# A two-layer decode kernel: three quarters of a single-head key cache loaded anew instead of four, PSUM laid out by hand, and the key products of five items shared among three engines

## The chip, the cores and the metric

The kernel runs on one core of one Trainium2 chip. The metric is the device time of one execution in microseconds (us). The kernel before was timed in three runs: 2697.79, 2698.55 and 2700.42 us, so its median is 2698.55 us. An engine is named as in the profile: PE is TensorE, DVE is VectorE, ACT is ScalarE, POOL is GpSimd, and SP is the queue from which almost every DMA is issued.

## The reference

A residual stream of two tokens (batch 2, one position each, 576 wide) goes through the same two blocks twice: attention over a long cache, then a gated GELU block. The weights and the caches are the same in both layers, so each layer reads the whole key and value cache again.

```python
def _A_ref(x, k_cache, v_cache, wq, wo):          # H, Sk, Dh = 32, 8192, 128
    q = (lambda x, *d: x.transpose(*d))((x @ wq).reshape(B, Sq, H, Dh), 0, 2, 1, 3)
    scores = jnp.einsum("bhqd,bhkd->bhqk", q, k_cache) * (Dh ** -0.5)
    p = _softmax(scores, axis=-1)
    o = jnp.einsum("bhqk,bhkd->bhqd", p, v_cache)
    return (lambda x, *d: x.transpose(*d))(o, 0, 2, 1, 3).reshape(B, Sq, H * Dh) @ wo
def _B_ref(x, w_gate, w_up, w_down):
    g = jnp.einsum("bsd,df->bsf", x, w_gate)
    u = jnp.einsum("bsd,df->bsf", x, w_up)
    return jnp.einsum("bsf,fd->bsd", _gelu(g) * u, w_down)
x = A_x
x = x + _A_ref(_layernorm(x, axis=-1), A_k_cache, A_v_cache, A_wq, A_wo)
x = x + _B_ref(_layernorm(x, axis=-1), B_w_gate, B_w_up, B_w_down)
x = x + _A_ref(_layernorm(x, axis=-1), A_k_cache, A_v_cache, A_wq, A_wo)
x = x + _B_ref(_layernorm(x, axis=-1), B_w_gate, B_w_up, B_w_down)
```

Everything is float32. The key cache and the value cache hold 268 MB each.

## The kernel before

**Items and parts.** The attention of a layer is cut into 34 items (lines 60 to 65). Items 0 to 29 are pairs: two heads of one batch element, 8 MB (of 2^20 bytes) of keys and 8 MB of values. Items 30 to 33 (`SINGLE` in the code) are one head each, 4 MB of keys and 4 MB of values. An item is worked through in parts of 1 MB, that is 16 rows of 128 numbers on each of the 128 partitions: 8 parts in a pair, 4 in a single. A part is what the change calls a quarter of a key cache. Layer one takes the items from 0 to 33 (its code calls the layer 0), layer two from 33 down to 0 (layer 1 in the code).

**What a part costs.** `multiply` (line 520) multiplies the part in place by the query on DVE (line 527; the query was copied to all partitions by PE into PSUM, line 507). POOL then adds the right half of each row of 128 to its left half (line 539), and `add_up` (line 541) lets DVE sum the remaining 64 (line 542). In the first six items of layer two only 12 of the 16 rows go that way: ACT sums the other four, row by row (line 532, `own_rows` on line 512). `at_once` (line 516) marks the first and the last part of item 33 in layer two, which skip the POOL step, so that DVE sums whole rows. When `add_up` of a part is done, its place in SBUF is free, and the next load that waits for that place may start.

**Softmax and values.** After an item's last part, `peak` and `highest` find the maximum (DVE, then PE, then DVE, then PE), `softmax` takes the exponentials on ACT, `total` their sum (PE, reciprocal on DVE). `values` (line 617) multiplies the weights with the value cache on PE, 32 matmuls for a single and 64 for a pair, and frees a value part after every four groups of rows. `gather` (DVE), `context` (PE) and `divide` (DVE) make the output row. All of this is issued inside the parts of the next item, in the loop of lines 699 to 742: at k == 0 the last part of the previous item is added up, at k == 1 come `highest` and `softmax`, at k == 2 `total`, `gather` and `values`, at k == 3 `divide`. Each engine executes its own instructions strictly in the order in which they were written.

**Memory.** All loads go to one SBUF tile, `space`, cut into six slots of 4 MB, the last of which lies in a ring of four places. `plan_first`, `plan_second` and `plan_mlp` write down the order of all loads. They go out on SP in just that order, and each waits until what lay in its place is no longer needed. When layer one ends, the keys of items 32 and 33 and the values of items 31, 32 and 33 stay in SBUF for layer two (line 65). `plan_second` (line 343) then loads the query weights, the four key parts of item 31 into the ring, the four of item 30 over the keys of item 33, the values of item 30 over the values of item 33, the keys of item 29 over the keys and the values of item 32, the keys of item 28 in two halves of 4 MB into the slots 5 and 4, and the values of item 29 as one load of 8 MB into the slots 0 and 1. From then on keys and values alternate in loads of 8 MB.

**PSUM.** `acc` takes two of the eight banks of 2 KB per partition. `xps`, `po`, two buffers of `qp` (the query) and two of the small results (tag "small") are tiles of their own.

Of the kernel before, what the change touches and what calls it, by code (L numbers as in the profile page):

```python
# [9 lines left out]
F32 = mybir.dt.float32  # L10
# [112 lines left out]
def decode_layers(ctx, tc, x_in, kc, vc, wq, wo, wg, wu, wd, out):  # L123
# [6 lines left out]
    psum1 = ctx.enter_context(tc.tile_pool(name="psum1", bufs=1, space=PSUM))  # L130
    psum2 = ctx.enter_context(tc.tile_pool(name="psum2", bufs=2, space=PSUM))
    ctx.enter_context(tc.manual_schedule())
# [20 lines left out]
    def done(key):  # L153
        arena.free(key)
        pump()
# [187 lines left out]
    def plan_second():  # L343
        for us in WQ[1]:
            half_rows(("wq", 1, us[0]), wq, us, None)
        last = PAIRS - 1
        k63, v63, k62, v62 = ("k", 1, SINGLE[3]), ("v", 1, SINGLE[3]), ("k", 1, SINGLE[2]), ("v", 1, SINGLE[2])
        for k in range(4):
            one(("k", 1, SINGLE[1]), kc, SINGLE[1], k, None)
        for k in range(4):  # L350
            one(("k", 1, SINGLE[0]), kc, SINGLE[0], k, (k63, k))

        for kind, k in (("v", 0), ("v", 1), ("k", 0), ("v", 2), ("v", 3), ("k", 1), ("k", 2), ("k", 3)):
            if kind == "k":
# [12 lines left out]
        for g in groups(1):  # L367
            out_rows(1, g)
# [72 lines left out]
    nc.vector.memset(xps, 0.0)  # L441


    def norm(split=False):
# [5 lines left out]
        )  # L450
        every4 = psum2.tile([P, 4 * 6], F32, name="every4", tag="small")
        nc.tensor.matmul(every4, same, apart.rearrange("p c t -> p (c t)"), start=True, stop=True)
# [27 lines left out]
    def attention(layer):  # L480
# [13 lines left out]
        qb, S, prod, rs, mT, rinv, osb = {}, {}, {}, {}, {}, {}, {}  # L494
        po = psum1.tile([P, GH, 2], F32, name="po")

# [15 lines left out]
        def own_rows(n):  # L512

            return 12 if layer == 1 and n in seq[:6] else JC

        def at_once(n, k):

            return layer == 1 and n == seq[0] and k in (0, ITEMS[n].parts - 1)

        def multiply(n, k):  # L520

            if k == 0:
                S[n] = work.tile([P, SK * 2 // P], F32, name="S")
# [3 lines left out]
            nc.vector.tensor_tensor(  # L527
                out=u, in0=t, in1=qb[n].unsqueeze(1).to_broadcast([P, JC, DH]), op=ALU.mult
            )
            r = own_rows(n)  # L530
            for j in range(r, JC):
                nc.scalar.activation(  # L532
                    u[:, j, :], u[:, j, :], AF.Copy, accum_out=S[n][:, k * JC + j:k * JC + j + 1]
                )
# [4 lines left out]
            nc.gpsimd.tensor_tensor(out=half, in0=half, in1=u[:, :r, DH // 2:], op=ALU.add)  # L539

        def add_up(n, k):
            nc.vector.tensor_reduce(  # L542
                out=S[n][:, k * JC:k * JC + own_rows(n)], in_=prod.pop((n, k)), axis=AX.X, op=ALU.add
            )
# [6 lines left out]
            if k == ITEMS[n].parts - 1:  # L551
                ready.pop(key)

        def peak(n):
            m = work.tile([P, 1], F32, name="m")
            nc.vector.reduce_max(m, S[n][:, :ITEMS[n].rows], axis=AX.X)  # L556
            mT[n] = psum2.tile([1, P], F32, name="mT", tag="small")
            nc.tensor.transpose(mT[n], m, ident)  # L558

        def highest(n):  # L560

            heads = ITEMS[n].heads
            m1 = work.tile([1, 2], F32, name="m1")
            nc.vector.reduce_max(m1[:, :heads], mT.pop(n).rearrange("p (i q) -> p i q", i=heads), axis=AX.X)  # L564
            mT[n] = psum2.tile([P, 2], F32, name="nb", tag="small")
            nc.tensor.matmul(mT[n][:, :heads], ones[0:1, :], m1[:, :heads], start=True, stop=True)  # L566
# [28 lines left out]
        def total(n):  # L595
            it = ITEMS[n]
            tot = psum2.tile([P, 2], F32, name="tot", tag="small")
            nc.tensor.matmul(tot[:, :it.heads], ones, rs.pop(n), start=True, stop=True)  # L598
# [275 lines left out]
```

## Time and profile before

The profiled execution took 2699.86 us; the span from its first to its last instruction was 2698.0 us.

| | |
|---|---|
| median of three runs | 2698.55 us |
| profiled execution, its span | 2699.86 us, 2698.0 us |
| bytes moved by DMA | 1155.41 MB, mean 428 GB/s |
| DVE busy | 1865.5 us (69%) |
| POOL busy | 1189.3 us (44%) |
| PE busy | 897.0 us (33%) |
| ACT busy | 130.9 us (5%) |

The shares are means over stages that differ: two attention stages of some 1200 us each, and two short blocks of weights. The page has a row that shows for each of 40 slices how busy the 16 DMA engines were and how much they moved; that row is to be read first, then the same for shorter windows, then the instructions inside the windows that stand out.

### The profile page before, as it was taken

What the parts mean: (1) busy time and instruction counts of PE and PEld (TensorE: products, weight loads), DVE (VectorE), ACT (ScalarE), POOL (GpSimd) and SP (SyncE); (2) the same over time, 40 slices, a digit from 0 to 9 for tenths busy, and PEclk for the clock granted to TensorE, in tenths of its full rate; (3) what the DMA queues carried; (4) which work ended last, traced back from release to release, by engine and by line L of the source; (5) the groups of instructions that cost most, each with busy time, mean ns of one, the idle gap of its engine ahead of it and who ended that gap; (6) DMA issues with size and microseconds to landing.
All of it is one profiled execution on the core that took longest, in us unless ns stands there. A gap on an engine that the chain in (4) does not pass through costs nothing.

```text
span 2698.0 us, 18267 instructions
## 1 busy us (share of the span) xinstructions
PE 897.0 (33%) x7020; PEld 293.9 (11%) x7020; DVE 1865.5 (69%) x1688; ACT 130.9 (5%) x657; POOL 1189.3 (44%) x526
## 2 busy tenths in 40 slices
PE   1323332333233223334653332333233323322355
PEld 0100010001000000111211110001000100000022
DVE  4877787678777776876039887778767867787740
ACT  0000000000000000000013100000000000000000
POOL 2644454445445444544015454445444544544420
PEclk7656665665666566666666665666566666656667
DMA  9999999999999999999999999999999999999998
GB/s 420 436 433 433 434 435 433 432 433 435 434 433 433 432 432 432 433 429 422 407 388 409 434 428 433 433 435 431 432 435 434 431 435 432 434 434 434 435 420 379
DMA packets 33687, 1155.41 MB, mean 428 GB/s; under 512 B 4008, under 2 KB 4032, under 8 KB 5824
## 3 DMA queue, kind: packets, MB, share of 16 engines
q1 hardware_dynamic: 33560, 1154.24, 99.5%
q8 instruction: 55, 0.90, 0.1%
q14 instruction: 32, 0.26, 0.0%
q10 hardware_dynamic: 40, 0.01, 0.0%
HBM read 1154.23 MB, written 0.00 MB: 428 GB/s over the span
## 4 chain that ended last, share of the span: by engine, by line
DMA 84%; DVE 13%; PE 2%; issue 1%; POOL 0%; SPq 0%; ACT 0%; ACTq 0%; DVEq 0%; POOLq 0%
DMA space<-in_A_k_cache_dram 75%; DVE space L527 8%; DVE S L542 4%; DMA space<-in_B_w_up_dram 3%; DMA space<-in_A_wo_dram 2%; DMA space<-in_A_v_cache_dram 2%; DMA space<-in_B_w_down_dram 2%; DMA space<-in_A_wq_dram 1%; PE acc L628 0%; POOL space L539 0%; DMA space<-in_B_w_gate_dram 0%; PE acc L782 0%; DMA x<-in_A_x_dram 0%; PE acc L487 0%; PE xps L831 0%
## 5 line engine op out<-in xcount | busy, mean ns | idle before, releaser
L539 POOL TENSOR_TENSOR space<-space 128x1024 f32<-128x1024 f32 (+1 forms) x510 | 1185.3, 2324 | 1269.1 <-DVE space L527 1253.2
L527 DVE TENSOR_TENSOR space<-space,qp 128x2048 f32<-128x2048 f32 x512 | 1166.3, 2278 | 597.1 <-DMA space<-in_A_k_cache_dram 571.8
L628 PE MATMUL acc<-space,prz 128*8 128x512 f32 x4096 | 589.0, 738 | 455.7 <-DMA space<-in_A_v_cache_dram 450.9
L542 DVE TENSOR_REDUCE S<-space 128x16 f32<-128x1024 f32 (+1 forms) x512 | 612.4, 1196 | 3.1 <-POOL space L539 3.1
L558 PE MATMUL mT<-ident,m 128*1 128x128 f32 x68 | 25.0, 367 | 806.0 <-DVE m L556 806.0
L628 PEld LDWEIGHTS acc<-space,prz 128*8 128x8 f32 x4096 | 118.0, 103 | 869.4 <-DMA space<-in_A_v_cache_dram 451.8
L587 ACT ACTIVATE nbs<-nb 64x1 f32<-64x1 f32 (+1 forms) x128 | 21.1, 165 | 2230.7 <-PE nb L566 2230.0
L558 PEld LDWEIGHTS mT<-ident,m 128*1 128x1 f32 x68 | 5.4, 79 | 822.9 <-issue 791.7
L653 PE MATMUL po<-of,osb 128*32 128x2 f32 x512 | 41.0, 202 | 130.8 <-DVE osb L644 130.8
L566 PE MATMUL nb<-m,unit 1*128 1x2 f32 (+1 forms) x136 | 39.4, 357 | 124.9 <-DVE m L564 124.9
L473 POOL TENSOR_TENSOR rstd<-ve,mhalf 128x1 f32<-128x1 f32 x4 | 2.2, 550 | 167.0 <-DVE ve L471 167.0
L644 DVE SCALAR_TENSOR_TENSOR osb<-acc,diag,osb 128x128 f32<-128x128 f32 x192 | 67.4, 351 | 6.8
L807 DVE STREAM_TRANSPOSE o<-o 128x288 f32<-128x288 f32 x4 | 2.8, 693 | 92.4 <-ACT o L805 92.4
L598 PE MATMUL tot<-sums,unit 128*128 128x2 f32 x120 | 35.3, 363 | 91.7 <-ACT prz L589 91.7
L507 PE MATMUL qp<-qsb,pick 4*64 4x128 f32 (+1 forms) x256 | 31.3, 306 | 80.1 <-DVE space L527 76.9
L589 ACT ACTIVATE prz<-S,nbs 64x128 f32<-64x128 f32 (+1 forms) x128 | 50.7, 396 | 11.7 <-POOL prz L579 7.5
L653 PEld LDWEIGHTS po<-of,osb 128*32 128x32 f32 x512 | 35.7, 154 | 139.1 <-DVE osb L644 137.8
L566 PEld LDWEIGHTS nb<-m,unit 1*128 1x128 f32 x136 | 33.5, 304 | 146.3 <-DVE m L564 146.3
L477 DVE TENSOR_TENSOR x<-xps,x 128x144 f32<-128x144 f32 x4 | 1.2, 308 | 69.0 <-PE xps L831 39.1
L532 ACT ACTIVATE space<-space 128x128 f32<-128x128 f32 x128 | 38.0, 297 | 64.5 <-DVE space L527 60.8
L598 PEld LDWEIGHTS tot<-sums,unit 128*128 128x128 f32 x120 | 30.1, 312 | 96.9 <-ACT prz L589 96.9
L782 PE MATMUL acc<-space,xt 128*8 128x288 f32 x288 | 31.4, 581 | 18.4 <-DMA space<-in_B_w_up_dram 10.7
(64 smaller groups left out, 345.6 us busy)
## 6 DMA issues: line engine op xcount, KB each, us to landing
space<-in_A_k_cache_dram SPq DMA_DIRECT2D x6, 4096.0 KB
space<-in_A_v_cache_dram SPq DMA_DIRECT2D x6, 4096.0 KB
space<-in_A_wo_dram SPq DMA_DIRECT2D x15, 1152.0 KB
space<-in_A_k_cache_dram SPq DMA_DIRECT2D x16, 1024.0 KB
space<-in_B_w_gate_dram SPq DMA_DIRECT2D x3, 3456.0 KB
space<-in_A_v_cache_dram SPq DMA_DIRECT2D x10, 1024.0 KB
space<-in_A_wq_dram SPq DMA_DIRECT2D x3, 3072.0 KB
space<-in_B_w_gate_dram SPq DMA_DIRECT2D x16, 576.0 KB
```

The costliest lines, as they stand in the source:

```text
L507: nc.tensor.matmul(qb[n][to, :], pick[32 * c:32 * c + 4, r:r + 1].to_broadcast([4, P // it.heads]), qsb[32 * c:32 * c + 4, (h % 4) * DH:(h ...
L527: nc.vector.tensor_tensor(out=u, in0=t, in1=qb[n].unsqueeze(1).to_broadcast([P, JC, DH]), op=ALU.mult)
L532: nc.scalar.activation(u[:, j, :], u[:, j, :], AF.Copy, accum_out=S[n][:, k * JC + j:k * JC + j + 1])
L539: nc.gpsimd.tensor_tensor(out=half, in0=half, in1=u[:, :r, DH // 2:], op=ALU.add)
L542: nc.vector.tensor_reduce(out=S[n][:, k * JC:k * JC + own_rows(n)], in_=prod.pop((n, k)), axis=AX.X, op=ALU.add)
L566: nc.tensor.matmul(mT[n][:, :heads], ones[0:1, :], m1[:, :heads], start=True, stop=True)
L589: nc.scalar.activation(pr[at, lo:].rearrange("p (g e) -> p g e", e=4)[:, 0:it.rows // 2:2, :], s[at, :it.rows].rearrange("p (g r) -> p g r ...
L598: nc.tensor.matmul(tot[:, :it.heads], ones, rs.pop(n), start=True, stop=True)
L628: nc.tensor.matmul(accumulator(n)[32 * c:32 * c + 8, :], pr[:, at:at + 8], t[g // 4][:, g % 4 * 4:g % 4 * 4 + 4, :].rearrange("p j d -> p ...
L644: nc.vector.scalar_tensor_tensor(t, q[:, r, :], diag[:, r:r + 1], t, op0=ALU.mult, op1=ALU.add,)
L653: nc.tensor.matmul(po[lo:lo + 32, i, :], t[:, i::GH], of, start=True, stop=True)
L782: nc.tensor.matmul(acc[32 * c:32 * c + 4 * B, h, :HG], window(u, 4 * g + 2 * e), w[:, k, c, :], start=(key == steps[0][0] and k == 0), sto ...
```

## The change

It has five parts.

1. While layer one works on item 31, ACT copies the item's last key part into four banks of PSUM (`kept`) before it is overwritten by the products. In layer two only three key parts of item 31 are loaded; when its first part has been added up, ACT copies `kept` into that part's place, and it is used from there as the fourth part.
2. `plan_second` follows: the ring's fourth place takes the first key part of item 30, every later load of the stage is moved up by one place, and the values of item 29 are loaded in two halves, each of which waits for its own slot only.
3. For the first five items of layer two (33, 32, 31, 30, 29) DVE multiplies 12 of the 16 rows of each part; POOL multiplies the other four with a copy of the query that ACT has put in SBUF. ACT now sums seven rows of each part instead of four, and POOL and DVE sum nine instead of twelve (in the two parts done at once: ACT five, DVE eleven). The sixth item, 28, is no longer treated in a special way.
4. PSUM, with four banks gone, is laid out by hand: `xps` and both query buffers share one bank, `po` and both small buffers another. The query of the next item is issued after the first `multiply` of an item instead of ahead of it.
5. Where the item before the current one is a single, `divide` is put off from k == 3 to k == 1 of the next item (`late`); elsewhere it stays at k == 3.

```diff
-        for k in range(4):
+        for k in range(3):
             one(("k", 1, SINGLE[1]), kc, SINGLE[1], k, None)
         for k in range(4):
-            one(("k", 1, SINGLE[0]), kc, SINGLE[0], k, (k63, k))
-        for kind, k in (("v", 0), ("v", 1), ("k", 0), ("v", 2), ("v", 3), ("k", 1), ("k", 2), ("k", 3)):
+            one(("k", 1, SINGLE[0]), kc, SINGLE[0], k, (k63, k - 1) if k else None)
+        one(("k", 1, last), kc, last, 0, (k63, 3))
+        turns = iter(range(1, 5)), iter(range(4))
+        for kind in "vkvvkvkk":
             if kind == "k":
-                one(("k", 1, last), kc, last, k, (k62, k))
+                k = next(turns[0])
+                one(("k", 1, last), kc, last, k, (k62, k - 1))
             else:
+                k = next(turns[1])
                 one(("v", 1, SINGLE[0]), vc, SINGLE[0], k, (v63, k))
-        for k in range(4):
-            one(("k", 1, last), kc, last, 4 + k, (v62, k))
+        for k in range(5, 8):
+            one(("k", 1, last), kc, last, k, (v62, k - 5))
         half(("k", 1, last - 1), kc, last - 1, 0, 5)
         half(("k", 1, last - 1), kc, last - 1, 4, 4)
-        cache(("v", 1, last), vc, last)
+        half(("v", 1, last), vc, last, 0, 0)
+        half(("v", 1, last), vc, last, 4, 1)
...
-    xps = psum1.tile([P, CW], F32, name="xps")
+    bank = psum1.tile([P, 512], F32, name="bank")
+    xps = bank[:, 0:CW]
     nc.vector.memset(xps, 0.0)
+    qps = [bank[:, CW + i * DH:CW + (i + 1) * DH] for i in range(2)]
+    bank2 = psum1.tile([P, 512], F32, name="bank2")
+    po = bank2[:, 0:2 * GH].rearrange("p (i c) -> p i c", c=2)
+    smalls = [bank2[:, 2 * GH + i * P:2 * GH + (i + 1) * P] for i in range(2)]
+    kept = psum1.tile([P, JC, DH], F32, name="kept")
...
-            qb[n] = psum2.tile([P, DH], F32, name="qp")
+            qps.append(qps.pop(0))
+            qb[n] = qps[0]
...
-        def own_rows(n):
-            return 12 if layer == 1 and n in seq[:6] else JC
+        def waited(n):
+            return layer == 1 and n in seq[:5]
+        def own_rows(n, k):
+            return 11 if at_once(n, k) else 9 if waited(n) else JC
+        qs = once.tile([P, 2, DH], F32, name="qs", tag="xc")
...
             u = t = ready[name("k", layer, n)][k]
+            if n == SINGLE[1] and k == 3 and layer == 0:
+                nc.scalar.copy(kept, t)
...
+            rows = 12 if waited(n) else JC
             nc.vector.tensor_tensor(
-                out=u, in0=t, in1=qb[n].unsqueeze(1).to_broadcast([P, JC, DH]), op=ALU.mult
+                out=u[:, :rows, :], in0=t[:, :rows, :], in1=qb[n].unsqueeze(1).to_broadcast([P, rows, DH]), op=ALU.mult
             )
-            r = own_rows(n)
+            if rows < JC:
+                q = qs[:, n % 2, :]
+                if k == 0:
+                    nc.scalar.copy(q, qb[n])
+                nc.gpsimd.tensor_tensor(
+                    out=u[:, rows:, :], in0=t[:, rows:, :], in1=q.unsqueeze(1).to_broadcast([P, JC - rows, DH]),
+                    op=ALU.mult,
+                )
+            r = own_rows(n, k)
...
             key = name("k", layer, n)
+            if layer == 1 and n == SINGLE[1]:
+                if k == 0:
+                    ready[key][3] = ready[key][0]
+                    nc.scalar.copy(ready[key][3], kept)
+                    return
+                k = k % 3
             done((key, k))
...
+        late = None
         for i, n in enumerate(seq):
             last = i == N - 1
-            if not last:
-                query(seq[i + 1])
...
             if first:
+                query(seq[i + 1])
                 add_up(p, ITEMS[p].parts - 1)
...
                 multiply(n, k)
+                if k == 0 and not last and not first:
+                    query(seq[i + 1])
...
-                if k == 3 and a is not None:
+                if k == 3 and a is not None and p < PAIRS:
                     divide(a)
+                if k == 1 and late is not None:
+                    divide(late)
+            late = a if a is not None and p >= PAIRS else None
```

More of the change, by code (lines that the diff above doesn't have):

```diff
@@ L130, in decode_layers @@
     psum1 = ctx.enter_context(tc.tile_pool(name="psum1", bufs=1, space=PSUM))
-    psum2 = ctx.enter_context(tc.tile_pool(name="psum2", bufs=2, space=PSUM))
     ctx.enter_context(tc.manual_schedule())
@@ L439, in decode_layers, with small @@
         nc.vector.memset(acc[:, s, :], 0.0)
-    xps = psum1.tile([P, CW], F32, name="xps")
+    bank = psum1.tile([P, 512], F32, name="bank")
+    xps = bank[:, 0:CW]
     nc.vector.memset(xps, 0.0)
+    qps = [bank[:, CW + i * DH:CW + (i + 1) * DH] for i in range(2)]
[3 more added lines that the diff above has]
+    kept = psum1.tile([P, JC, DH], F32, name="kept")
+    def small(p, n):
+        smalls.append(smalls.pop(0))
+        return smalls[0][0:p, 0:n]
     def norm(split=False):
@@ L450, in norm @@
         )
-        every4 = psum2.tile([P, 4 * 6], F32, name="every4", tag="small")
+        every4 = small(P, 4 * 6)
         nc.tensor.matmul(every4, same, apart.rearrange("p c t -> p (c t)"), start=True, stop=True)
@@ L494, in attention @@
         qb, S, prod, rs, mT, rinv, osb = {}, {}, {}, {}, {}, {}, {}
-        po = psum1.tile([P, GH, 2], F32, name="po")
         oT = once.tile([P, H // GH, GH, 2, B], F32, name="oT", tag="part")
@@ L542, in add_up @@
             nc.vector.tensor_reduce(
-                out=S[n][:, k * JC:k * JC + own_rows(n)], in_=prod.pop((n, k)), axis=AX.X, op=ALU.add
+                out=S[n][:, k * JC:k * JC + own_rows(n, k)], in_=prod.pop((n, k)), axis=AX.X, op=ALU.add
             )
@@ L549, in add_up @@
             key = name("k", layer, n)
+            if layer == 1 and n == SINGLE[1]:
[4 more added lines that the diff above has]
+                k = k % 3
             done((key, k))
-            if k == ITEMS[n].parts - 1:
+            if k == ITEMS[n].parts - 1 or not any(c == key for c, _ in arena.live):
                 ready.pop(key)
@@ L556, in peak @@
             nc.vector.reduce_max(m, S[n][:, :ITEMS[n].rows], axis=AX.X)
-            mT[n] = psum2.tile([1, P], F32, name="mT", tag="small")
+            mT[n] = small(1, P)
             nc.tensor.transpose(mT[n], m, ident)
@@ L564, in highest @@
             nc.vector.reduce_max(m1[:, :heads], mT.pop(n).rearrange("p (i q) -> p i q", i=heads), axis=AX.X)
-            mT[n] = psum2.tile([P, 2], F32, name="nb", tag="small")
+            mT[n] = small(P, 2)
             nc.tensor.matmul(mT[n][:, :heads], ones[0:1, :], m1[:, :heads], start=True, stop=True)
@@ L596, in total @@
             it = ITEMS[n]
-            tot = psum2.tile([P, 2], F32, name="tot", tag="small")
+            tot = small(P, 2)
             nc.tensor.matmul(tot[:, :it.heads], ones, rs.pop(n), start=True, stop=True)
```

## The prediction

> **What bounds the kernel now.** I read the page first: busy shares, the 40 slices, the chain.
>
> ```profile
> span 2698.0 us, 18267 instructions
> ...
> PE 897.0 (33%) x7020; PEld 293.9 (11%) x7020; DVE 1865.5 (69%) x1688; ACT 130.9 (5%) x657; POOL 1189.3 (44%) x526
> ...
> GB/s 420 436 433 433 434 435 433 432 433 435 434 433 433 432 432 432 433 429 422 407 388 409 434 428 433 433 435 431 432 435 434 431 435 432 434 434 434 435 420 379
> ...
> DMA 84%; DVE 13%; PE 2%; issue 1%; POOL 0%; SPq 0%; ACT 0%; ACTq 0%; DVEq 0%; POOLq 0%
> ```
>
> No engine is full; memory is. The transfers run at 432 to 435 GB/s and sag in slices 18 to 22. At 434 GB/s a part (1.0486 MB) takes 2.42 us. So a change can gain only by moving fewer bytes or by filling the sag. Next I read windows of 10 us there; the last two columns are the DMA share and GB/s.
>
> ```profile
> 1400.00:1410.00 10.00, 1.40 (x5) 0.84 (x5) 9.43 (x9) 3.83 (x24) 3.63 (x2) 0.50 0.74 270
> 1410.00:1420.00 10.00, 6.20 (x36) 1.48 (x36) 7.11 (x5) 3.18 (x19) 3.65 (x2) 0.75 0.96 354
> ...
> 1430.00:1440.00 10.00, 6.67 (x40) 2.03 (x40) 9.96 (x8) 4.85 (x33) 6.09 (x4) 0.72 0.99 376
> ...
> 1460.00:1470.00 10.00, 6.82 (x34) 1.29 (x34) 10.00 (x9) 3.99 (x25) 5.51 (x4) 0.67 0.83 330
> ```
>
> Here layer two begins. DVE (third pair) is full while DMA runs dry: loads wait for places that computing frees. In whole: the last query weights are in at 1391.16 (PE starts on them), the keys of item 27 at 1508.66 (DVE starts). Between lie 44 parts, 44 x 2.42 = 106.3 of 117.5 us, so 11.2 us are lost. Afterwards DMA never starves until the tail: in steady state DVE waits 9.55 us for the keys of an item.
>
> Then the timeline, for what a part costs.
>
> ```profile
> 1464.49 2.26 DVE L527 TENSOR_TENSOR space<-space,qp 128x2048 f32<-128x2048 f32 x1
> ...
> 1466.68 0.93 DVE L542 TENSOR_REDUCE S<-space 128x12 f32<-128x768 f32 x1
> ...
> 1466.90 1.81 POOL L539 TENSOR_TENSOR space<-space 128x768 f32<-128x768 f32 x1 [1.29 <-DVE space L527]
> 1466.94 0.33 SPq L166 DMA_DIRECT2D space<-in_A_v_cache_dram  x1
> 1467.10 0.29 ACT L532 ACTIVATE space<-space 128x128 f32<-128x128 f32 x1
> ...
> 1467.55 2.27 DVE L527 TENSOR_TENSOR space<-space,qp 128x2048 f32<-128x2048 f32 x1
> ```
>
> One part every 3.06 us, all DVE: 2.19 to the next start for the product, 0.87 for the sum; POOL and ACT (0.295 a row) wait. The SP row is the load of item 29's values, held back by DVE's and PE's work on item 30 until 1466.94: that is the dip of the last window.
>
> **The change part by part.**
>
> Bytes: one part less. 2.4 us off a stream that is otherwise full. The extra loads of halves cost one SP issue (0.33 us), beside running transfers.
>
> The copy to PSUM in layer one: ACT, 2048 wide. No row shows it; from ACT's 128x128 (297 ns) and 128x288 (497 ns) rows, 1.25 ns an element and 0.14 fixed, it is 2.7 us at most; with the slope of 128x256 (470 ns) to 128x288, 0.84 ns, 2.0. I take 2.1; from below nothing, where it lies in a wait. It is issued behind softmax of item 30, which ends at 1219.98, so ends at 1222.1; DVE wants the fourth part at 1223.27. Hidden; at 2.7 still. What is behind it on ACT is the softmax of item 31, 16 us later. The copy back in layer two stands on ACT between the rows of item 31's second and third part, and DVE and POOL wait for it before the fourth: about 1.5 us once, in a stretch with slack (below).
>
> The part in the first five items of layer two. DVE's price per element from its two sums (1.21 for 1024, 0.94 for 768) is 1.05 ns: the product of 1536 takes 2.19-0.54=1.65, the sum of 576 0.87-0.20=0.67, so 2.32. ACT: 7 rows x 0.295=2.07. POOL: its adds take 2.356 (1024) and 1.816 (768), so 2.1 ns an element and 0.20 fixed: the add of 576 is 1.41. The product of 512 is in no row. Lower end 1.28, if it costs as an add; upper end 2.4, if twice that slope (POOL's one other arithmetic on tensors, a power of one element, is 0.55 and mostly fixed cost). I take 1.28: same instruction, float32, two SBUF inputs. POOL then sets the pace, 2.69 us a part against 3.06.
>
> The shared bank: PE may write the next query only after DVE's product and ACT's copy of the query, and the next product waits for that. In steady state it is 0.45 to 0.8 us of PE under 1.4 us of DVE's sum and maximum; if uncovered it eats from the 9.55 us of waiting. The Trainium skill's page "PSUM — Partial Sum Buffer", section "PSUM bank collisions raise a hardware error", speaks against this layout: engines must be kept apart by bank, not by address, even two readers. By that rule the waits are real; the sum above has them.
>
> In layer two PE's order makes it longer once: at item 29 the query of 28 stands behind the values of item 31 (6.2 us), and the next product starts some 2 us late. In place of it the wait of the old `divide` goes (2.83 us of DVE at 1453.96), put off by the fifth edit. In layer one that edit frees 2.16 us of DVE where it then waits for keys anyway: nothing.
>
> Now the loads, with these prices, from the first product at 1394.57 (place freed, before in brackets). Item 33: 1399.2 (1398.7; ACT's rows now end behind POOL's product), 1401.9 (1404.0), 1404.5 (1407.0), 1406.2 (1408.7). Its values start 2.35 later as now, 1408.5, and free the first place 1.96 on, 1410.4 (1413.0). DVE then waits for PE, as now: the values take 5.57, so item 32's first sum ends at 1415.3 (1418.05). A load starts some 2 us after issue: one issued at 1403.98 meets shares of 0.30, 0.53 and 0.91 in the 2-us windows from 1402. Four parts run to 1400.9; then the queue is dry for 0.3, 0.3, 0.2, 0, 1.0 and 2.5 us, together 4.3. From 1417.3 it stays filled: 19 parts end near 1441.5; the keys of 28 go out at 1437.5 (1440.0) and, behind the values of item 31, near 1448 (1453.6), needed by 1449; the values of 29 near 1451.5 and 1456.5 (1466.9), needed by 1459; the keys of 27 near 1470 (1483.0), needed by 1478. Parts of 1 MB run at 422 to 426, 0.06 us more each, 1.2. Lost: 5.5 in place of 11.2, 5.7 less. The same reckoning gives only 9.4 of the 11.2 for the kernel before; I charge half of the missing 1.8 here, so 4.8 less.
>
> Sum: 2.4 + 4.8 = 7.2 us. From there on everything comes 7.2 earlier; the tail is unchanged. The span goes from 2698.0 to 2690.8; the median lies 0.55 above that span, and I keep this: 2691.4.
>
> **The rivals.**
>
> Only the bytes. The early gaps stay: the first five places are freed in a chain through PE and ACT that POOL's extra product only lengthens (the first place is later already), and the load of 28's second half misses its 1 us of margin. For it: values of 5.6 and 6.2 us are untouched. Against it: the dip at 1460 goes with the split load, which has 7 us of margin. Gain 0 to 5: about 2695.
>
> Slower: POOL's product costs more than the add. The place is items 33 to 29, 24 parts. A part takes 1.41 plus the product. At 2.0 it is 0.72 longer than forecast, and the some 12 parts up to the values of item 31, which free the place for the second half of 28, come 8.6 us later, of which 1 is margin: the gain of 7.2 is gone. At 2.4, the upper end, 12 x 0.4 = 5 us more: about 2704. For it: POOL now does two instructions a part in strict order, and waits for ACT's copy at each item. Against it: its adds do not slow beside DVE's products (1.81 here, 1.816 mean). The page "GPSIMD Engine Reference", section "Performance versus the Vector engine", has 4497 ns for an add of 2048, an estimate of 1.12 for 512, and advises elementwise work on VectorE; the row agrees on the price, and by it the forecast stands.
>
> Larger: the early gaps close wholly, 2.4 + 8 = 10 us, 2688.
>
> That a part is not saved: excluded, since the list of loads in the changed program has 15 single-part key loads in layer two in place of 16.
>
> **How the numbers follow.** Forecast 0.57, only the bytes 0.22, slower 0.15, larger 0.06. A measurement of this kernel tells about 0.2%, 5.4 us, from no change. The forecast's own spread, 5 to 9 us, lies above that for nine tenths: faster 0.52 + 0.06 = 0.58; same: 0.05 of the forecast and all of the bytes case, 0.27; slower 0.15. Range: from 2688.3 to 2699.5, which leaves out most of the slower case and a little below; the forecast's own is 2689 to 2694.
>
> **What would show it.** Right: 1154.4 MB; POOL products near 1.28 us and parts every 2.7 in 1420 to 1470; the window 1460 to 1470 at 430 GB/s; the keys of item 27 in DVE near 1501.4; a wait of some 4 us at the reciprocal near 1411, unchanged steady state at 38.7 us an item. Wrong: POOL products over 2 us, DMA dry after 1430, or a longer period per item, which would mean that the shared bank reaches the steady state.

## The result, and the profile after

| | before | after |
|---|---|---|
| median of 14 runs each | 2698.56 us | 2693.03 us |
| lowest and highest | 2697.6, 2700.87 | 2690.76, 2695.51 |
| profiled execution, its span | 2699.86, 2698.0 | 2693.42, 2691.6 |
| first product of item 33 in DVE | 1394.57 | 1394.98 |
| first product of item 27 in DVE | 1508.66 | 1502.43 |

The medians are 5.5 us apart. The ratio over all runs is 0.9978, with a 95% interval of 0.9971 to 0.9985, which is 5.9 us (4.0 to 7.8): the changed kernel is faster. The prediction was 2691.4 us, which is 1.6 us less than was measured. In the two profiled executions the span is 6.4 us shorter; 7.2 were forecast.

The page of the changed kernel, the same rows as were shown of before:

```profile
span 2691.6 us, 18179 instructions
...
PE 919.8 (34%) x7020; PEld 302.3 (11%) x7020; DVE 1850.8 (69%) x1688; ACT 145.6 (5%) x736; POOL 1213.8 (45%) x550
...
GB/s 421 436 435 434 433 431 435 429 435 434 432 435 433 434 433 429 433 429 426 407 397 416 435 434 436 434 430 436 430 433 434 435 432 433 436 433 430 430 426 374
DMA packets 33687, 1154.36 MB, mean 429 GB/s; under 512 B 4008, under 2 KB 4032, under 8 KB 5824
...
DMA 79%; PE 12%; DVE 7%; POOL 1%; issue 1%; ACT 0%; SPq 0%; ACTq 0%; POOLq 0%; DVEq 0%
```

One part less is moved (1155.41 MB before). POOL is 24.5 us busier and DVE 14.7 us less. Slices 20 to 22 (1279 to 1480 us) are still low ones, 407, 397 and 416 GB/s where they were 407, 388 and 409. From slice 23 on the two rows agree within 6 GB/s, and from the first product of item 27 to the end the span has 1189.3 us before and 1189.2 after: what was gained was gained at the start of layer two.

The windows at the start of layer two, and the whole stretch of 110 us (columns: PE, PE's weight loads, DVE, ACT, POOL busy with their instructions, PE's granted clock, DMA share, GB/s):

```profile
1400.00:1410.00 10.00, 2.71 (x13) 1.35 (x17) 8.83 (x10) 7.03 (x45) 5.52 (x5) 0.50 0.94 358
1410.00:1420.00 10.00, 4.82 (x34) 0.97 (x23) 6.55 (x7) 6.40 (x42) 8.76 (x7) 0.84 0.79 295
1430.00:1440.00 10.00, 5.75 (x35) 1.48 (x27) 9.15 (x9) 9.03 (x61) 8.54 (x8) 0.67 1.02 421
1460.00:1470.00 10.00, 0.90 (x5) 0.37 (x5) 9.72 (x10) 7.37 (x48) 9.48 (x8) 0.53 1.06 454
1390.00:1500.00 110.00, 46.46 (x269) 16.12 (x261) 89.99 (x88) 58.08 (x354) 79.09 (x55) 0.62 0.98 411
```

For the last of these rows the kernel before has:

```profile
1390.00:1500.00 110.00, 46.09 (x253) 16.69 (x257) 97.04 (x83) 41.36 (x252) 49.29 (x28) 0.61 0.96 391
```

Three of the four windows are fuller than before: 358 GB/s where it was 270, 421 for 376, 454 for 330. One is emptier: 1410 to 1420 has 295 in place of 354. Over the 110 us it is 411 in place of 391, and in this time POOL works 79 us in place of 49, ACT 58 in place of 41, DVE 90 in place of 97.

The empty window is explained by the timeline of DVE there:

```profile
1409.65 1.75 DVE L554 TENSOR_TENSOR space<-space,bank 128x1536 f32<-128x1536 f32 x1 [0.33 <-ACT qs L560]
1414.86 0.17 DVE L648 RECIPROCAL rinv<-bank 128x1 f32<-128x1 f32 x1 [3.45 <-PE bank L640]
1414.94 0.74 DVE L577 TENSOR_REDUCE S<-space 128x9 f32<-128x576 f32 x1
1415.59 1.75 DVE L554 TENSOR_TENSOR space<-space,bank 128x1536 f32<-128x1536 f32 x1
```

The reciprocal waits 3.45 us for PE's sum of the exponentials, which PE does only after the values of item 33 (they stand ahead of it in PE's order and take 5.47 us). The sum of item 32's first part stands behind the reciprocal on DVE, so that part's place comes free late, and the next load of keys goes out only at 1415.74. The wait was there before, too (2.90 us, until 1416.97).

From item 27 on the two kernels are alike: DVE waits some 9.6 to 9.8 us for the keys of an item in both (single items more, up to 10.7), and one item follows the other after 38.7 to 38.9 us.

### The profile page after: what moved, and what is told of

Same layout as the page of the kernel before. It is cut to its first block, busy times and chain, and to the rows that moved or that the text cites. A ratio compares the mean times of both kernels' runs of the same rounds, so it can differ in the third digit from the quotient of the medians.

```text
span 2691.6 us, 18179 instructions
## 1 busy us (share of the span) xinstructions
PE 919.8 (34%) x7020; PEld 302.3 (11%) x7020; DVE 1850.8 (69%) x1688; ACT 145.6 (5%) x736; POOL 1213.8 (45%) x550
## 4 chain that ended last, share of the span: by engine, by line
DMA 79%; PE 12%; DVE 7%; POOL 1%; issue 1%; ACT 0%; SPq 0%; ACTq 0%; POOLq 0%; DVEq 0%
DMA space<-in_A_k_cache_dram 40%; DMA space<-in_A_v_cache_dram 32%; PE acc L670 10%; DVE space L554 4%; DMA space<-in_B_w_down_dram 2%; DVE S L577 2%; DMA space<-in_B_w_gate_dram 2%; DMA space<-in_A_wo_dram 1%; DMA space<-in_B_w_up_dram 1%; POOL space L574 1%; DMA space<-in_A_wq_dram 1%; PE bank L878 0%; PE acc L829 0%; POOL space L561 0%; DMA x<-in_A_x_dram 0%
## 5 line engine op out<-in xcount | busy, mean ns | idle before, releaser
L554 DVE TENSOR_TENSOR space<-space,bank 128x2048 f32<-128x2048 f32 (+1 forms) x512 | 1153.6, 2253 | 604.7 <-DMA space<-in_A_k_cache_dram 576.5
L525 PE MATMUL bank<-qsb,pick 4*64 4x128 f32 (+1 forms) x256 | 47.0, 439 | 777.9 <-DVE space L554 765.6
L695 PE MATMUL bank<-of,osb 128*32 128x2 f32 x512 | 40.9, 202 | 130.9 <-DVE osb L686 130.9
L608 PE MATMUL bank<-m,unit 1*128 1x2 f32 (+1 forms) x136 | 39.2, 355 | 129.5 <-DVE m L606 129.5
L640 PE MATMUL bank<-sums,unit 128*128 128x2 f32 x120 | 35.2, 363 | 92.2 <-ACT prz L631 92.2
L695 PEld LDWEIGHTS bank<-of,osb 128*32 128x32 f32 x512 | 35.7, 154 | 139.1 <-DVE osb L686 137.9
L608 PEld LDWEIGHTS bank<-m,unit 1*128 1x128 f32 x136 | 33.3, 303 | 149.2 <-DVE m L606 149.2
L600 PE MATMUL bank<-ident,m 128*1 128x128 f32 x68 | 25.0, 368 | 72.0 <-DVE m L598 72.0
L561 POOL TENSOR_TENSOR space<-space,qs 128x512 f32<-128x512 f32 x24 | 30.4, 1268 | 30.8 <-ACT qs L560 30.8
L640 PEld LDWEIGHTS bank<-sums,unit 128*128 128x128 f32 x120 | 30.0, 310 | 97.3 <-ACT prz L631 97.3
```

The costliest lines, as they stand in the source:

```text
L525: nc.tensor.matmul(qb[n][to, :], pick[32 * c:32 * c + 4, r:r + 1].to_broadcast([4, P // it.heads]), qsb[32 * c:32 * c + 4, (h % 4) * DH:(h ...
L554: nc.vector.tensor_tensor(out=u[:, :rows, :], in0=t[:, :rows, :], in1=qb[n].unsqueeze(1).to_broadcast([P, rows, DH]), op=ALU.mult)
L561: nc.gpsimd.tensor_tensor(out=u[:, rows:, :], in0=t[:, rows:, :], in1=q.unsqueeze(1).to_broadcast([P, JC - rows, DH]), op=ALU.mult,)
L695: nc.tensor.matmul(po[lo:lo + 32, i, :], t[:, i::GH], of, start=True, stop=True)
```

## The experiments

Ratios are to the kernel before, run on the same chip in turn with the experiment, with their 95% intervals. "Stage" is the time from DVE's first product of item 33 to that of item 27 in one profiled execution; it was 114.1 us before and 107.5 after. The changed kernel itself, run a second time, shows how well this can be read:

> The changed kernel once more, on the same chip as the three others, as what they are compared with: 2693 within 1 us, 7 us lost between the query weights and the keys of item 27.

Measured: 2693.22 us (2691.32 to 2695.74), ratio 0.9977 (0.9969 to 0.9986), stage 108.9. So this median repeats within 0.2 us, but that is one repeat: the kernel before has 2698.56, 2698.8, 2698.99 and 2699.77 us in the four sets in which it was timed. Medians of different sets can therefore be compared to about 1 us, no better. The stage of a single execution varies by 1.4 us. The windows vary with it (249 GB/s in 1410 to 1420, again the lowest, where it was 295), so that a difference of less than some 50 GB/s in one window of one execution says little by itself.

A second measure is used below, too: the time from PE's start on the last query weights to DVE's start on the keys of item 27. It was 117.5 us before, 110.84 after and 111.25 in this repeat. It leaves out when the stage begins, which differs from profile to profile. After it, twelve of the thirteen profiled executions take 1188.6 to 1190.0 us to the end, and the slowest kernel 1186.5.

**Without POOL's share.** All of the change, but the rows are shared out as before:

```diff
         def waited(n):
-            return layer == 1 and n in seq[:5]
+            return False
...
         def own_rows(n, k):
-            return 11 if at_once(n, k) else 9 if waited(n) else JC
+            return 12 if layer == 1 and n in seq[:6] else JC
```

> The changed kernel without its third part: DVE multiplies all 16 rows again, ACT sums four rows of a part in the first six items of layer two, as before; the kept quarter, the order of loads, the split values of item 29 and the PSUM layout stay. Additive theory (a part less is worth 2.4 us by itself, the sharing only shortens the early gaps, the split load closes the dip at 1460): 4 to 5 us faster than before, near 2694. Rival, not additive (the early loads wait for places that computing frees, so a load less only makes the queue run dry sooner, until compute has caught up): about 2 us faster, near 2696.5, with about as much lost between the query weights and the keys of item 27 as before (11 us) although a part less is loaded. The trace tells them apart: when DVE starts on the keys of item 27 (1508.66 before, 1502.43 in the changed kernel).

Measured: 2698.1 us (2695.57 to 2699.16), ratio 0.9995 (0.9986 to 1.0004), stage 112.2. That is slower than either theory of the expectation had it. The windows of this kernel:

```profile
1400.00:1410.00 10.00, 1.16 (x3) 0.57 (x3) 9.43 (x8) 3.84 (x24) 3.63 (x2) 0.50 0.76 256
1410.00:1420.00 10.00, 6.73 (x36) 1.80 (x36) 6.77 (x6) 3.17 (x19) 3.64 (x2) 0.67 0.75 278
...
1460.00:1470.00 10.00, 5.49 (x32) 0.88 (x32) 10.00 (x8) 3.84 (x24) 5.57 (x4) 0.81 1.00 429
1390.00:1500.00 110.00, 47.99 (x269) 16.64 (x261) 99.14 (x85) 44.28 (x261) 50.59 (x29) 0.62 0.96 394
```

The kept quarter, the new order of loads, the split load, the new PSUM layout and the late `divide`, all together and without the share, are worth 0.7 us by the medians. The interval goes from 3.8 faster to 1.1 slower, so it includes nothing, and it includes the 2.42 us that a part takes to load. The profile shows why the part need not count in full here: DVE is as full as before (99 of 110 us), places come free no sooner, and the queue runs dry for longer. From PE's last query weights (1391.69) to the keys of item 27 (1507.34) it is 115.65 us with 43 parts, 103.9 of them moving at 434 GB/s; 11.7 are lost, where it was 11.2 with 44 parts. And the window of 1460 is filled (429 GB/s for 330), but the total is nearly as it was: the gap is now in the two windows from 1400 (256 and 278 GB/s, 270 and 354 before).

**POOL's share alone.** The kernel before with the third part of the change only:

```diff
+            rows = 12 if waited(n) else JC
             nc.vector.tensor_tensor(
-                out=u, in0=t, in1=qb[n].unsqueeze(1).to_broadcast([P, JC, DH]), op=ALU.mult
+                out=u[:, :rows, :], in0=t[:, :rows, :], in1=qb[n].unsqueeze(1).to_broadcast([P, rows, DH]), op=ALU.mult
             )
+            if rows < JC:
...
+                nc.gpsimd.tensor_tensor(
...
+            r = own_rows(n, k)
```

> The kernel before with only the third part of the change: POOL multiplies four rows of each part of the first five items of layer two, ACT sums seven, POOL and DVE nine; all four key parts of item 31 are loaded, and order of loads, PSUM tiles, place of the query and of divide are those of before. Additive theory: the changed kernel's 6.2 us less the byte part of 2.4, so 3 to 4 us faster, near 2695. Rival, not additive (computing frees the places, the queue is what it waits for): nearly all of the gain, 5 to 6 us, near 2693, with only some 2 us of DMA dry instead of 4, and keys of item 27 in DVE near 1503.

Measured: 2693.8 us (2692.38 to 2695.8), ratio 0.9981 (0.9972 to 0.9990), stage 110.2. The windows of this kernel:

```profile
1400.00:1410.00 10.00, 4.59 (x21) 1.66 (x25) 8.33 (x8) 6.60 (x43) 5.66 (x5) 0.50 0.99 372
1410.00:1420.00 10.00, 3.27 (x24) 1.10 (x16) 7.45 (x8) 7.12 (x47) 8.27 (x7) 0.84 0.99 363
...
1460.00:1470.00 10.00, 0.69 (x4) 0.29 (x4) 9.47 (x8) 7.91 (x50) 9.48 (x9) 0.57 1.03 443
1390.00:1500.00 110.00, 45.88 (x265) 14.59 (x265) 90.12 (x88) 56.27 (x353) 79.01 (x55) 0.64 1.01 422
```

The share alone is worth 5.0 of the 5.5 us. (The third part also gives ACT three more rows of each part and ends the special treatment of item 28; no run separates these from POOL's four rows.) DVE falls from 97 to 90 us in the stretch, places come free sooner, and the transfers run at 422 GB/s. From the last query weights (1390.84) to the keys of item 27 (1503.3) it is 112.46 us with 44 parts, and 6.2 are lost in place of 11.2: the same 5.0 us.

The whole change, with one part less to move, is emptier in the window from 1410 (295 GB/s, here 363) and loses 6.9 and 7.4 us in its two profiles. The stretch of the whole change is still the shorter one, by 1.6 and 1.2 us. The profiled totals, 2693.67 here and 2693.42 there, hide this, since the stage began 1.9 us earlier here (1393.08 against 1394.98). The window of 1460 is full here with the values of item 29 loaded as one piece: it needs no split.

**The layout alone.** The changed kernel without the share, the kept part, and the new order of loads with its split load; the shared banks, the later query and the late `divide` remain. Two of the places edited:

```diff
-    kept = psum1.tile([P, JC, DH], F32, name="kept")
...
-            if n == SINGLE[1] and k == 3 and layer == 0:
-                nc.scalar.copy(kept, t)
```

> The changed kernel without the kept quarter, without its order of loads and without POOL's share: what is left of the change are the shared PSUM banks, the query issued after the first product, and the put-off divide. If the shared banks cost nothing in the steady state, as the prediction has it: item after item 38.7 us, and at most the 2.83 us wait of the old divide to gain in the early stage, some of which reaches the queue: 0 to 2 us faster than before, 2697 to 2699. If the waits between PE and DVE on one bank reach the queue: slower by 0.1 us an item or more, over 2701.

Measured: 2698.62 us (2697.53 to 2699.76), ratio 0.9997 (0.9988 to 1.0006), stage 113.5. Of the start of layer two one window, and of its steady state two neighbouring items in DVE:

```profile
1460.00:1470.00 10.00, 4.88 (x32) 0.75 (x23) 10.00 (x9) 3.84 (x24) 5.46 (x3) 0.67 1.07 436
```

```profile
2011.85 2.29 DVE L546 TENSOR_TENSOR space<-space,bank 128x2048 f32<-128x2048 f32 x1 [9.75 <-DMA space<-in_A_k_cache_dram]
...
2050.61 2.29 DVE L546 TENSOR_TENSOR space<-space,bank 128x2048 f32<-128x2048 f32 x1 [9.74 <-DMA space<-in_A_k_cache_dram]
```

The items are 38.76 us apart, and before each DVE still waits 9.7 us for memory. The bank that both queries share with `xps` costs nothing that can be measured, over the items of both layers. The dip at 1460 is gone in this kernel as well (436 GB/s, 330 before), with neither the share nor the split, and the time is the same as before: that one window doesn't tell what the time does.

**A dearer product on POOL.** The slower rival turned on what POOL's product costs. Two kernels make it dearer by one or two further products of two rows into unused space, ahead of POOL's own. The edit for one (for two, `range(2)`):

```diff
+                spare = part_at(END - 2 * DH, 2 * DH).rearrange("p (j d) -> p j d", d=DH)
+                for _ in range(1):
+                    nc.gpsimd.tensor_tensor(
+                        out=spare, in0=t[:, rows:rows + 2, :], in1=q.unsqueeze(1).to_broadcast([P, 2, DH]), op=ALU.mult
+                    )
```

> The changed kernel with one more product of 256 on POOL (results not used) ahead of each of its products in the five items: about 0.72 us more a part, 3.4 us in all, which is the point at which the prediction has the gain gone (products of 2.0 together). With two such products the kernel took 2714.84, 21.8 more than the changed kernel for 24 parts. If POOL's pace sets the stage from there on: 2698 to 2701, level with before. If some of POOL's time still lies under DVE's and PE's: 2693 to 2696.

> The changed kernel with two more products of 256 on POOL ahead of each of its products in the five items; their results are not used. They cost about 0.74 us each, so a part costs POOL 4.15 instead of 2.67 us. The prediction's slower rival put the point from which POOL decides at a product of 2.0 us; here the products together take 2.75. If POOL's pace sets the early stage: 24 parts, of which some 12 count until the second half of item 28's keys, so 8 to 16 us slower than before, 2707 to 2715. If DVE and PE set it and POOL has slack: within 2 us of the changed kernel.

Measured: with one, 2699.02 us (2696.19 to 2699.99), ratio 0.9997 (0.9988 to 1.0006); with two, 2714.84 us (2713.4 to 2716.94), ratio 1.0059 (1.0046 to 1.0071). POOL's groups with two of them (busy us, mean ns, idle time before):

```profile
L579 POOL TENSOR_TENSOR space<-space 128x1024 f32<-128x1024 f32 x488 | 1150.3, 2357 | 1191.1 <-DVE space L554 1175.1 <-DVE m L611 11.2 <-issue 3.3
L563 POOL TENSOR_TENSOR space<-space,qs 128x256 f32<-128x256 f32 x48 | 34.9, 728 | 29.7 <-ACT qs L560 27.8
...
L566 POOL TENSOR_TENSOR space<-space,qs 128x512 f32<-128x512 f32 x24 | 30.5, 1271 | 1.9
```

DVE's sums, all 512 of the kernel, from the pages: with one further product, then with two.

```profile
L582 DVE TENSOR_REDUCE S<-space 128x16 f32<-128x1024 f32 (+1 forms) x512 | 609.8, 1191 | 14.0 <-POOL space L579 14.0
```

```profile
L582 DVE TENSOR_REDUCE S<-space 128x16 f32<-128x1024 f32 (+1 forms) x512 | 610.0, 1192 | 29.8 <-POOL space L579 29.8
```

The product's price is 1.27 as it is, 2.00 with one more and 2.73 with two. At 2.00 the gain is gone, just where the rival had its threshold. A second 0.73 costs 15.8 us more by the medians (16.7 by the ratios): POOL is now the pace of the stage, 24 parts x 0.73 = 17.5 us, and nearly all of it shows. The first 0.73 cost only 6.0 (5.1 by the ratios), since a part of it filled POOL's slack. DVE's sums say it directly: in the changed kernel they wait 3.0 us for POOL in all, with one product more 14.0, with two 29.8. The first product adds 11.0 us of waiting and 6.0 to the time, the second 15.8 to both.

**The order on PE.** In the changed kernel the sum of the exponentials of the first item (33) is put ahead of its values:

```diff
                 if k == 1 and first:
+                    total(p)
                     values(v)
-                    total(p)
```

> The changed kernel with one pair of lines exchanged: after the first item of layer two the sum of its weights goes to PE ahead of its 32 value matmuls instead of behind them. In the changed kernel DVE waits 3.45 us for that sum, until 1414.86, and the load of item 29's second key part goes out at 1415.74, when the queue has run dry. If that wait is the cause of the 1410 to 1420 dip (295 GB/s): DVE goes on near 1411, the load goes out near 1413, the dip shrinks by 2 to 2.6 us and the time falls by as much, to about 2690.5. If the dip comes from the places of the values, which PE frees one by one, or from the late start of a load: no change within 1 us.

Measured: 2691.86 us (2690.36 to 2693.35), ratio 0.9972 (0.9962 to 0.9983), stage 107.7. DVE at the same place:

```profile
1409.72 1.75 DVE L554 TENSOR_TENSOR space<-space,bank 128x1536 f32<-128x1536 f32 x1 [0.34 <-ACT qs L560]
1411.39 0.16 DVE L648 RECIPROCAL rinv<-bank 128x1 f32<-128x1 f32 x1
```

The wait of 3.45 us is gone, and the key load that went out at 1415.74 goes out at 1413.27; the window from 1410 rises from 295 to 347 GB/s. The median is 1.2 us lower than the changed kernel's, but the intervals overlap: it isn't shown that this beats it.

**The order of loads as well.** The same, and keys and values in the ring in another order:

```diff
-        for kind in "vkvvkvkk":
+        for kind in "vvkvkvkk":
```

> The changed kernel with the sum of item 33's weights ahead of its values on PE, as in the run before, and with the loads of item 30's first two value parts side by side (v v k v k v k k instead of v k v v k v k k), so that the second does not stand on the queue behind a key part whose place comes free later. If the queue still runs dry for lack of issued loads near 1415 (347 GB/s in the run with the exchange alone): the 1410 to 1420 window rises to 400 or more, another 0.5 to 1.5 us, near 2691. If what is left is the rate of separate loads of 1 MB: the same as with the exchange alone, within 0.7 us.

> The kernel with both exchanges (sum of the weights ahead of the values, first two value parts side by side) once more, since 2691.63 against 2693.22 for the changed kernel lay within their intervals. If the closed dip is what made the difference: again 2691 to 2692.3, and 105 to 107 us from DVE's first product of item 33 to its first of item 27. If it was chance: 2693.

Measured: 2691.63 us (2690.63 to 2693.77) and 2691.98 us (2690.72 to 2694.05), both with a ratio of 0.9973 (0.9963 to 0.9983 and 0.9984); stages 106.2 and 107.5. The windows of the first, then the early one of the second:

```profile
1410.00:1420.00 10.00, 5.70 (x33) 0.96 (x22) 8.54 (x9) 8.24 (x52) 9.77 (x9) 0.67 0.95 377
...
1390.00:1500.00 110.00, 48.16 (x261) 16.38 (x261) 90.13 (x88) 58.04 (x354) 79.21 (x55) 0.61 1.00 417
```

```profile
1410.00:1420.00 10.00, 5.67 (x32) 0.94 (x24) 8.54 (x9) 8.24 (x53) 9.85 (x8) 0.67 0.93 349
```

The early window reaches 377 GB/s in the first and 349 in the second, where 400 or more were expected and the exchange on PE alone had 347: the other order of loads is not seen to do anything. With the 2691.86 of the exchange alone these are the three lowest medians of the study, 1.0 to 1.4 us below the changed kernel's 2693.03. But each interval holds the others' ratio, and the next kernel, which has neither exchange, comes to 2692.18. A gain in time from the two orders is not shown.

**The values of item 29 as one load again**, in the changed kernel:

```diff
-        half(("v", 1, last), vc, last, 0, 0)
-        half(("v", 1, last), vc, last, 4, 1)
+        cache(("v", 1, last), vc, last)
```

> The changed kernel with the values of item 29 as one load of 8 MB again, which waits for both slots. In the changed kernel the halves go out at 1451.89 and 1458.58 and the queue is filled until about 1461, so the whole load would go out at 1458.6. If the prediction's reading is right that POOL's share alone has already closed the dip at 1460 to 1470: no difference, within 0.7 us of the changed kernel, and 1460 to 1470 at 430 GB/s or more. If the split closes the dip: 2 us slower, and a window below 400 GB/s there.

Measured: 2692.18 us (2690.71 to 2693.45), ratio 0.9974 (0.9965 to 0.9984), stage 107.1. The load in SP's queue, and the window that was the dip before:

```profile
1456.65 0.33 SPq L165 DMA_DIRECT2D space<-in_A_v_cache_dram  x1
```

```profile
1460.00:1470.00 10.00, 1.06 (x5) 0.37 (x5) 9.72 (x9) 6.31 (x41) 9.42 (x7) 0.50 1.05 454
```

The split is worth nothing that can be measured once DVE is relieved. The load goes out at 1456.65, ten microseconds earlier than in the kernel before (1466.94), because the work on item 30 ends earlier, and the queue does not run dry.

**The share with the exchanged order, no kept part**: the kernel of the second experiment with the edit of the fifth.

> The kernel before with the third part of the change alone (POOL's share) and the sum of item 33's weights ahead of its values: four key parts of item 31 are loaded, nothing is kept in PSUM. The run with POOL's share alone took 2693.8. If computing is the limit and the part less counts only when the queue never runs dry: the stage between the query weights and the keys of item 27 now loses some 4 to 5 us here, and the kernel with the kept quarter and the same exchange (2691.86) is ahead by most of a part, 1.5 to 2.4 us; so here near 2693.5. If the kept quarter is worth nothing: 2691.9, the same as with it.

Measured: 2695.33 us (2693.25 to 2696.95), ratio 0.9986 (0.9977 to 0.9994), stage 108.8. This was to tell what the kept part is worth when the early gap is closed. The kernels with the kept part and the exchange on PE have 2691.63 to 2691.98, which is 3.4 to 3.7 us less. That is more than the 2.42 a part can take, and this kernel came out 1.5 us above the same one without the exchange (2693.8), so a part of the difference is scatter. In its profile the stage began at 1396.40 and in the second experiment's at 1393.08, though the code ahead of it is the same; why is open.

The stretch from the last query weights to the keys of item 27 is freer of this. It is 112.46 and 112.19 us in the two kernels with the share and all 44 parts (the second experiment and this one), and 109.58 to 111.25 in the six profiles of kernels with the share and the kept part. These have the new layout and order of loads, too. By this the kept part is worth 0.9 to 2.9 us beside the share, and by the medians 0.6 to 3.7. So it seems to count there, and how near it comes to a whole part is open.

## Why the prediction was right, and where it was not

The sign, the place and the mechanism were right, and the time is 1.6 us from the forecast. In the stretch that the prediction added up, from the last query weights to the keys of item 27, 7.2 us were to be gained; the profiled execution gained 6.7 (117.5 to 110.84) and the repeat 6.2. The median gained 5.5. Medians of the kernel before lie up to 1.2 us apart, so no run assigns the rest to a term. That the total came so near is in part luck: the 4.8 for the gaps is 5.7 less half of 1.8 us that the reckoning couldn't place, a choice that no row supports.

**The bytes, 2.4 us: not settled.** The step reads "one part less. 2.4 us off a stream that is otherwise full". The stream is not full where the part was taken out: in 1410 to 1420 the changed kernel has 295 GB/s, 249 in its repeat, 297 with the values of item 29 whole and 278 without the share, while the three kernels with all parts and the old order on PE have 332 to 363. A load less can make the queue run dry earlier there in place of ending the stage earlier. Without the share, the first experiment gives 0.7 us for everything else, and 11.7 us are lost with 43 parts as 11.2 were with 44, so most of the term seems not to show; its interval does not exclude 2.4. Beside the share the part counts for 0.9 to 2.9 us in the stretch. The prediction worked out its loads with the part already gone, so its sum can hold; what the runs do not bear out is a price of 2.4 for the part by itself.

**The gaps, 4.8 us: right in size.** The share alone gives 5.0 (2.7 to 7.6 by its interval), and 5.0 less are lost in its stretch. In the whole change 6.9 and 7.4 us are lost where the prediction worked out 5.5 and charged 6.4. The gain comes from where it was put: DVE, 2.32 us a part. This price holds to the digit; two neighbouring products:

```profile
1454.47 1.74 DVE L554 TENSOR_TENSOR space<-space,bank 128x1536 f32<-128x1536 f32 x1
...
1456.79 1.74 DVE L554 TENSOR_TENSOR space<-space,bank 128x1536 f32<-128x1536 f32 x1
```

"POOL then sets the pace, 2.69 us a part" is half right. POOL's products follow each other at 2.66 us in the mean (five of them from 1449.85 to 1460.48), but DVE does not wait for them. The groups of the changed kernel:

```profile
L574 POOL TENSOR_TENSOR space<-space 128x576 f32<-128x576 f32 x22 | 30.9, 1406 | 3.5 <-DVE space L554 3.4
L561 POOL TENSOR_TENSOR space<-space,qs 128x512 f32<-128x512 f32 x24 | 30.4, 1268 | 30.8 <-ACT qs L560 30.8
L577 DVE TENSOR_REDUCE S<-space 128x9 f32<-128x576 f32 x22 | 16.4, 745 | 0.3 <-POOL space L574 0.2
...
L550 ACT COPY kept<-space 128x2048 f32<-128x2048 f32 x1 | 1.9, 1856 | 0.0
L589 ACT COPY space<-kept 128x2048 f32<-128x2048 f32 x1 | 1.8, 1844 | 0.0
```

The product of 512 costs 1.268 (1.28 taken, at the lower end of its bounds, because it is the same kind of instruction as the add); the add 1.406 (1.41). DVE's 22 sums wait 0.2 us for POOL in all: its parts of 2.32 and its other work between them come to about the same as POOL's. That is why one more product of 0.73 could still lie partly in slack. (Of POOL's 30.8 us of waiting for the query's copy, 23.15 lie ahead of its first product.) The estimate of 1.12 from the Trainium skill's page "GPSIMD Engine Reference", section "Performance versus the Vector engine", is 0.15 below the trace for this size; the measurement decides.

**The copies: hidden, as said, and cheaper.** 1.86 and 1.84 us, under the bounds of 2.0 to 2.7 that the smaller ACT rows gave, and under the 2.1 that was taken: the copy of 2048 has 0.9 ns an element. The first started at 1220.04 and ended at 1221.9, ahead of DVE's product at 1223.43. The copy back makes DVE wait 0.28 us, not 1.5.

**The shared bank: right.** In the steady state it costs nothing that can be measured, by the third experiment. Ahead of item 29's second product DVE waits 1.36 us for PE (2 forecast), in place of the old `divide`'s 2.83.

**The table of loads: right to about half a microsecond, but for one.** The four places of item 33's parts let loads go at 1399.75, 1402.45, 1404.99 and 1406.72 (1399.2, 1401.9, 1404.5 and 1406.2 worked out); the first value place at 1410.98 (1410.4), item 32's first at 1415.74 (1415.3). Later the keys of 28 at 1437.77 and 1448.27 (1437.5, 1448), the values of 29 at 1451.89 and 1458.58 (1451.5, 1456.5: the second half is 2.1 late), the keys of 27 at 1469.41 (1470). Most of the half microsecond is what the whole stage of this execution starts late (0.41). The keys of 27 reached DVE at 1502.43 for 1501.4. The loads could be forecast; of the 1.0 us that the keys of 27 came late, 0.4 is the late start. Their load went out 0.6 before its time, so the rest arose in the transfers; no run says where.

**The rivals.** "Only the bytes" named the right weak place (the chain through the values of item 33) and drew the wrong conclusion from it: by the first two experiments the share without the bytes gives 5.0 us, and the bytes without the share hardly anything that can be told from nothing. The prediction also held that the dip at 1460 goes with the split load; it is gone with the split, with the share and with neither, and the time doesn't follow it. "Slower" had its threshold right, a product of 2.0 us, but in part by luck: it set a cost of 7.6 us against a gain of 7.2, and the runs have 6.0 against 5.5. Beyond the threshold its price is too small: from 2.00 to 2.73 its 12 parts would cost 8.8 us, and the runs show 15.8, which is 0.73 for 21.6 of the 24 parts. "Larger" did not come: the gaps don't close, 6.9 us stay lost.

## What to carry to other kernels

A byte less need not be worth its transfer time where the queue is not full; look in short windows at the place from which it is taken, and where loads wait for places, relieve the engine that frees them first. A window that fills up is not yet a gain: the dip at 1460 closed in kernels that were no faster. A second engine can take a share of the pacing engine's work as long as its whole sequence for a part stays below the pace; test the margin by giving it one more instruction of known length. When a gap is closed, look for the next wait in the same chain (here the sum behind the values on PE). Compare small differences with how far the same kernel's medians lie apart, 1.2 us here.

## What the runs showed of the hardware that was not expected

- GpSimd's `tensor_tensor` in float32 goes by one line for products and sums: 0.73 us for 256 elements a partition, 1.27 for 512, 1.41 for 576, 2.36 for 1024, that is 0.19 us and 2.1 ns an element. DVE's products did not slow beside it: 1.74 us for 1536, where three quarters of the 2.28 for 2048 are 1.71.
- ScalarE's copy of 2048 float32 between SBUF and PSUM takes 1.84 to 1.86 us in both directions, 0.9 ns an element, where its activations have 2.3 ns at 128 (297 ns) and 1.8 at 256 (470 ns).
- The moment at which layer two's attention starts differs by 3.3 us between two profiles with the same code ahead of it (1393.08 and 1396.40), and the total moves with it. What makes this was not tried.
